# Negative maxima placed between down sums, a sum placed ahead of gelu's end, five places in each early section, and w_down loaded first

## The chip, the cores and the metric

The kernel runs on one core of a Trainium2 chip. The metric is the device time of one execution in microseconds (us). The core has five engines that run side by side and meet at semaphores: TensorE (PE in the profile, its weight loads PEld) multiplies matrices into PSUM, which has eight banks; VectorE (DVE), ScalarE (ACT) and GpSimd (POOL) work element by element; SyncE (SP) issues the DMAs here. Before the change the median of three runs is 2544.03 us (2543.72 to 2545.23).

## The reference

The input x is 2048 tokens of 576 values. One normalised copy of it feeds an attention block of 32 heads of 18 values and a GEGLU feed-forward block of 4608 hidden values. The result joins both:

```python
def _A_ref(x, wqkv, wo):
    ...
    scores = jnp.einsum("bhqd,bhkd->bhqk", q, k) * (Dh ** -0.5)
    p = _softmax(scores, axis=-1)
    o = jnp.einsum("bhqk,bhkd->bhqd", p, v)
    return (lambda x, *d: x.transpose(*d))(o, 0, 2, 1, 3).reshape(B, S, D) @ wo

def _B_ref(x, w_gate, w_up, w_down):
    return (_gelu(x @ w_gate) * (x @ w_up)) @ w_down

xn = _layernorm(x, axis=-1)
s = _A_ref(xn, A_wqkv, A_wo)
g = _silu(_B_ref(xn, B_w_gate, B_w_up, B_w_down))
return x + s * g
```

All inputs are float32. The kernel keeps that precision by splitting a value into a high part, rounded to the type fp32r that TensorE multiplies, and a low part, the rest.

## The kernel before

**Stages.** A prologue normalises x, transposes it and computes queries, keys and values into DRAM. Then come 144 sections (n = 0 to 143), and an epilogue that projects the attention's output and applies the gate.

**A section** (`section`) computes gate and up of 128 hidden values for one block of 512 tokens (`gate_up`): 27 pairs of matmuls, one on each half of the array's rows, into the PSUM tiles pg and pu. Other matmuls are spread between the pairs (`specials`). After it `activate` begins gelu: a square on ScalarE (L426), the product L427 on VectorE, and then, in the list `FF["rest"]`, `times` (a copy of pu on ScalarE, L435, and the product L438, which is the last to read pg) and `rest` (the tanh on ScalarE, L443, and gelu's last product L446 on VectorE). `finish` splits the hidden values into hh and hl, and after each second section it splits the two rows of w_down into dh and dl.

**A down product** (`down`, `half_downs`) multiplies the hidden values of two sections with their rows of w_down. It is cut into sums of 128 tokens by 288 columns, each accumulated in a PSUM tile py of one bank and then added by VectorE to the tile Y (`add_down`, L461; in the first rows of a block it is copied). Up to section 11 a run has four sums, two runs for each pair of sections; in the attention part it has eight, once for two sections. A sum is made of two halves, one on each half of the array; `behind` sets a mark on ScalarE after an opening half. The pieces of `FF["rest"]` are taken off at such marks, `times` at that of sum 0 and `rest` at that of sum `late` (1, or 2 in the last pair of a block).

**Attention** runs in 32 units (a block of 512 queries and four heads), four sections to a unit (n = 10 to 137, `ATT`). Before the exponentials the kernel needs the maximum of each row of scores, so the scores are multiplied twice: `max_mm` (L709, pm) with a maximum by VectorE (L712), and, five sections behind it, `score_mm` (L747, pe) with the exponential by ScalarE (L748). Eight slots of 32 make a section. `values` (L782, acc) runs after each second section. The first 40 slots of maxima lie ahead of the attention part, in the early sections: `FIRST` gives how many slots, called places here, each of the sections 0 to 9 takes. The last maximum of such a section waits until after L427 (`late`).

When the maxima of a unit are complete, `max_neg` forms the negative maxima on VectorE (L724), rounds them (the copy L725), subtracts to get the low part (L726), transposes both (L727) and stores them to DRAM (L728, mT). `max_rows` reads them back as rows of the query tiles (L736), so that the score matmul itself subtracts the maximum. In the attention part `max_neg` stands after each fourth section (12, 16, and so on to 132), ahead of that section's down product, and `max_rows` one section on. For the first unit both stand after section 8.

**Order.** The order on TensorE is that of the program text. On the other engines and on SP the build chooses an order by the text and the dependencies. Three helpers bind it: `tc.keep_in_program_order` and `kept` fix an instruction at its place, and `no_sync(a, b, ...)` puts a behind b on the engine without a semaphore; `after` is a real wait. SP is one queue, so a DMA that waits holds all behind it.

**Banks.** `BANKS` gives the eight banks to three tags: two to "f" (pg and pu), three to "m" (pm and acc) and three to "s" (pe). The sums of a down product borrow them: four sums as "smss", eight as "mmsmfmss".

**w_down.** `load_down` loads the rows of w_down for two sections when the second of them begins (L540). In the early sections its buffer is one of those of the exponentials (`lead_raw`).

## Time and profile before

| | |
|---|---|
| median of 3 runs | 2544.03 us (2543.72 to 2545.23) |
| the profiled execution | 2543.24 us |
| its span, first to last instruction | 2541.4 us |
| granted TensorE clock | 1.0 in the whole span |
| instructions | 63721 |
| DMA | 325.54 MB, 128 GB/s mean |

The page cuts the span into 40 slices and gives the busy share of each in tenths:

```profile
PE   9999999999999999999999999999999999999999
DVE  5316978888888888888888888888888888887277
ACT  3223467666667766667666667666666666676622
POOL 2127644555565554445565554554446555455575
PEclk9999999999999999999999999999999999999999
```

A slice is 63.5 us. The prologue takes the first three, the early sections lie in slices 4 and 5 (196.8 to 293 us), the attention part reaches from there into slice 38. In views by instruction, "x" is a count, the figure ahead of the bar says shapes, and the words in brackets or behind the last bar tell what ended the idle time of the engine. In the chain of waits each row is a start, a duration and the work that the chain ran through.

### The profile page before, as it was taken

The page shows a single profiled execution, that of the slowest core. Times are in us where ns is not written, and L with a number is a line of the kernel's source. Part 1 is how long each engine was busy: PE and PEld are TensorE (multiplying, and loading weights), DVE is VectorE, ACT ScalarE, POOL GpSimd, SP SyncE. Part 2 cuts the span into 40 slices and gives each one's busy share as a digit, 9 for nine tenths or more (in the row PEclk, how much of TensorE's full clock was granted, in tenths as well). Part 3 has the DMA queues.
Part 4 walks back from the last instruction along what each step waited for, and adds up shares of the span by engine and source line. Part 5 has one row for each costly group of instructions (what it writes and reads, how often), then busy time and mean ns, then how long its engine had stood idle before and what let it go on. Part 6 is the DMA issues. An engine that isn't in the chain of part 4 may idle for free.

```text
span 2541.4 us, 63721 instructions
## 1 busy us (share of the span) xinstructions
PE 2534.5 (100%) x24214; PEld 2022.0 (80%) x24214; DVE 1947.5 (77%) x3491; ACT 1563.5 (62%) x3098; POOL 1320.0 (52%) x1447
## 2 busy tenths in 40 slices
PE   9999999999999999999999999999999999999999
PEld 8889977777778877777777777777777777777698
DVE  5316978888888888888888888888888888887277
ACT  3223467666667766667666667666666666676622
POOL 2127644555565554445565554554446555455575
PEclk9999999999999999999999999999999999999999
DMA  8875444444464444444455444344446444443483
GB/s 267 266 242 151 110 107 104 110 103 110 108 155 114 109 103 110 113 113 111 111 129 142 111 109 108 105 104 112 108 112 157 111 110 109 107 109 97 116 238 109
DMA packets 398688, 325.54 MB, mean 128 GB/s; under 512 B 117408, under 2 KB 309184, under 8 KB 398384
## 3 DMA queue, kind: packets, MB, share of 16 engines
q1 hardware_dynamic: 398384, 321.47, 48.8%
q8 instruction: 193, 3.16, 0.5%
q14 instruction: 111, 0.91, 0.1%
HBM read 266.63 MB, written 54.70 MB: 126 GB/s over the span
## 4 chain that ended last, share of the span: by engine, by line
PE 98%; ACT 1%; DVE 0%; POOL 0%; issue 0%; POOLq 0%; ACTq 0%
PE pg L413 29%; PE py L473 18%; PE acc L782 18%; PE pm L709 9%; PE pe L747 9%; PE po L180 7%; PE pu L413 6%; PE po L921 2%; ACT pT L748 1%; PE pt L241 0%; PE po L232 0%; DVE t L446 0%; POOL dl L113 0%; POOL hl L113 0%; ACT t L426 0%
## 5 line engine op out<-in xcount | busy, mean ns | idle before, releaser
L748 ACT ACTIVATE pT<-pe 128x512 f32<-128x512 f32 x2048 | 1153.4, 598 | 364.6 <-PE pm L709 224.0
L712 DVE TENSOR_REDUCE mx<-pm 128x1 f32<-128x512 f32 x2048 | 1250.2, 682 | 148.2 <-PE pm L709 146.0
L413 PE MATMUL pu<-xd,wh 64*128 64x512 f32 x2592 | 925.9, 390 | 0.2 <-DVE t L438 0.2
L413 PE MATMUL pg<-xd,wh 64*128 64x512 f32 x2592 | 925.7, 390 | 0.0
L709 PE MATMUL pm<-KS,q 64*128 64x512 f32 x2048 | 779.2, 387 | 0.0
L747 PE MATMUL pe<-q,KS 64*128 64x512 f32 x2048 | 775.6, 387 | 0.9 <-DVE Y L461 0.9
L413 PEld LDWEIGHTS pg<-xd,wh 64*128 64x128 f32 x2592 | 476.9, 184 | 110.3 <-POOL wh L106 19.3
L413 PE MATMUL pg<-xd,wl 64*128 64x512 f32 x1296 | 501.3, 387 | 0.0
L413 PE MATMUL pu<-xd,wl 64*128 64x512 f32 x1296 | 501.3, 387 | 0.0
L413 PEld LDWEIGHTS pu<-xd,wh 64*128 64x128 f32 x2592 | 477.0, 184 | 1.1 <-DVE t L438 0.6
L782 PE MATMUL acc<-pT,VS 128*32 128x512 f32 x4096 | 452.8, 594 | 0.0
L108 POOL TENSOR_TENSOR wl<-raw,wh 128x384 fp32r<-128x384 f32 x432 | 433.4, 1016 | 14.0
L106 POOL TENSOR_SCALAR hh<-t 128x512 fp32r<-128x512 f32 x128 | 79.1, 618 | 663.3 <-DVE t L446 648.6
L709 PEld LDWEIGHTS pm<-KS,q 64*128 64x128 f32 x2048 | 374.9, 184 | 25.4 <-DVE mx L712 1.3
L747 PEld LDWEIGHTS pe<-q,KS 64*128 64x128 f32 x2048 | 370.5, 184 | 22.6 <-DVE Y L461 1.9
L473 PE MATMUL py<-dh,hh 64*128 64x288 f32 (+1 forms) x2240 | 366.0, 293 | 0.2
L473 PE MATMUL py<-dl,hh 64*128 64x288 f32 (+1 forms) x2240 | 365.3, 292 | 0.1
L473 PE MATMUL py<-dh,hl 64*128 64x288 f32 (+1 forms) x2240 | 364.5, 292 | 0.0
L782 PEld LDWEIGHTS acc<-pT,VS 128*32 128x32 f32 x4096 | 127.3, 110 | 289.9 <-issue 278.4
L106 POOL TENSOR_SCALAR wh<-raw 128x384 fp32r<-128x384 f32 x432 | 217.2, 514 | 137.6 <-PE pu L413 82.7
L461 DVE TENSOR_TENSOR Y<-py,Y 128x288 f32<-128x288 f32 x544 | 226.1, 452 | 53.5 <-PE py L473 46.3
L413 PEld LDWEIGHTS pg<-xd,wl 64*128 64x128 f32 x1296 | 238.6, 184 | 30.3
(120 smaller groups left out, 3135.3 us busy)
## 6 DMA issues: line engine op xcount, KB each, us to landing
KS<-qk SPq DMA_DIRECT2D x1536, 36.0 KB
raw<-in_B_w_gate_dram SPq DMA_DIRECT2D x144, 288.0 KB
raw<-in_B_w_up_dram SPq DMA_DIRECT2D x144, 288.0 KB
raw<-in_B_w_down_dram SPq DMA_DIRECT2D x67, 576.0 KB
VS<-vs SPq DMA_DIRECT2D x128, 152.0 KB
qk<-t SPq DMA_DIRECT2D x72, 256.0 KB
q<-qk SPq DMA_DIRECT2D x384, 36.0 KB
xx<-in_A_x_dram SPq DMA_DIRECT2D x32, 288.0 KB
```

Of the source, the lines that this page charges most:

```text
L106: first = nc.gpsimd.tensor_scalar(hi, raw, 1.0, 1.0, op0=ALU.mult, op1=ALU.mult)
L108: low_part[:] = [keep(nc.gpsimd.tensor_tensor(lo, raw, f(hi), op=ALU.subtract))]
L180: nc.tensor.matmul(o, st, m, start=(i == 0), stop=(i == len(terms) - 1))
L413: nc.tensor.matmul(o, w[1 + wp][k][rr, c, :], xd[xp][k][rr, c, :], start=(i == 0), stop=(i == len(terms) - 1))
L461: one = kept(nc.vector.tensor_tensor(yy, py, yy, op=ALU.add))
L473: return nc.tensor.matmul(py, hs[g][a][rr, j * P:(j + 1) * P], wd[w][rr, g, 288 * c:288 * c + 288], start=start, stop=stop)
L709: nc.tensor.matmul(pm, QS[u, r][rr, t * P:(t + 1) * P], KS[(u * NA + c) % KB][r][rr, :], start=True, stop=True)
L712: return nc.vector.tensor_reduce(MX[u][:, 2 * r + a, t, c:c + 1], pm, axis=AX.X, op=ALU.max)
L747: nc.tensor.matmul(pe, KS[(u * NA + c) % KB][r][rr, t * P:(t + 1) * P], QS[u, r][rr, :], start=True, stop=True)
L748: nc.scalar.activation(PT[u, kt][:, 2 * r + a, :], pe, AF.Exp, scale=SCALE)
L782: nc.tensor.matmul(ACC[u][32 * a:32 * a + 32, :], VS[(u * NA + c) % VB][:, v:v + 32], pt[:, a, :], start=first, stop=last, skip_group_chec ...
L921: nc.tensor.matmul(po, parts_of(b, j)[x_][:, k, :], OW[w][c][k], start=(i == 0), stop=(i == len(OUT) - 1))
```

## The change

Four edits and what they need. The order of gelu's pieces is taken apart: `tanh` and `rest` are now two entries of `FF["rest"]`. `max_neg` returns its four steps in place of doing them; the second is a second reduction of the maxima into the rounded tile, where a copy stood. The steps wait in `FF["between"]`: in runs of eight sums one is taken off after the third sum and two after the fourth, and what is left goes behind the last sum (`downs`). In runs of four sums nothing is taken off between the sums, and all four steps go behind the last. In runs of four, gelu's last product stands behind the first sum and ahead of the second. `FIRST` gives five places to each of the sections 2 to 9, where it gave 4, 5, 5, 5, 5, 5, 5, 6. The first rows of w_down are asked for ahead of the first keys and queries. For the first unit `max_rows` moves from right behind `max_neg` to the section's end.

```diff
-FIRST = (0, 0, 4, 5, 5, 5, 5, 5, 5, 6)
+FIRST = (0, 0) + (5,) * 8
...
-        def rest(behind=None, evicted=None):
-            tanh = kept(nc.scalar.activation(t1, t1, AF.Tanh, scale=GC * GS))
+        def tanh(behind=None, _=None):
+            one = kept(nc.scalar.activation(t1, t1, AF.Tanh, scale=GC * GS))
             if behind:
-                no_sync(tanh, behind, "a mark first")
+                no_sync(one, behind, "a mark first")
+
+        def rest(_=None, evicted=None):
             one = kept(nc.vector.scalar_tensor_tensor(t1, t1, 1.0, t2 if early else pg, op0=ALU.add, op1=ALU.mult))
             if evicted:
                 no_sync(one, evicted, "a finished sum first")
             if not early:
                 kept(nc.vector.tensor_tensor(t1, t1, pu, op=ALU.mult))
-
-        return t1, [times, rest] if early else [rest]
+            return one
+
+        return t1, [times, tanh, rest] if early else [tanh, rest]
...
-            one = kept(nc.vector.tensor_tensor(yy, py, yy, op=ALU.add))
+            one = FF["added"] = kept(nc.vector.tensor_tensor(yy, py, yy, op=ALU.add))
...
                             if begun == 0:
                                 evicted = add_down(b, r, pys[k], Y, j, c)
+                                if ahead:
+                                    no_sync(evicted, ahead, "between two finished sums")
+                                    ahead = None
+                                done += 1
+                                if done == 1 and len(sums) == 4 and len(FF["rest"]) == 1:
+                                    ahead = FF["rest"].pop(0)(None, evicted)
+                                for _ in range({3: 1, 4: 2}.get(done, 0) if len(sums) > 4 and FF["between"] else 0):
+                                    ahead = FF["between"].pop(0)(evicted)
                             elif a == 1 or len(sums) == 4:
                                 seen[k] = behind(one)
                                 if k in (0, late) and FF["rest"]:
-                                    FF["rest"].pop(0)(seen[k], evicted if k == 2 else None)
+                                    FF["rest"].pop(0)(seen[k])
+                                if k == late and FF["rest"] and len(sums) > 4:
+                                    FF["rest"].pop(0)(None, evicted if k == 2 else None)
...
-            FF["rawd"] = load_down(r, raw_d() if raw_d else raw_tile([P, G, D])) if ahead else FF.pop("next_d")
+            FF["rawd"] = FF.pop("first_d") if n < G else load_down(r, raw_d() if raw_d else raw_tile([P, G, D])) if ahead else \
+                FF.pop("next_d")
...
     def downs():
         while FF["down"] and (FF["down"][0][-1] < FF["n"] or FF["n"] == NF):
             down(*FF["down"].pop(0)[:-1])
+        while FF["between"]:
+            FF["between"].pop(0)(FF["added"])
...
-        def max_neg(u, keep=lambda i: i):
+        def max_neg(u):
...
-            keep(nc.vector.tensor_reduce(nm, MX[u].rearrange("p a t c -> p (a t) c"), axis=AX.X, op=ALU.max, negate=True))
-            nc.vector.tensor_copy(m2[:, 0:MH], nm)
-            nc.vector.tensor_tensor(m2[:, MH:2 * MH], nm, f(m2)[:, 0:MH], op=ALU.subtract)
-            nc.vector.transpose(m2t, f(m2))
-            nc.sync.dma_start(mT[u], m2t)
+
+            def step(what):
+                def go(behind=None):
+                    one = what()
+                    if behind:
+                        no_sync(one, behind, "a finished sum first")
+                    return one
+                return go
+
+            def square():
+                one = nc.vector.transpose(m2t, f(m2))
+                nc.sync.dma_start(mT[u], m2t)
+                return one
+
+            return [step(what) for what in (
+                lambda: nc.vector.tensor_reduce(nm, MX[u].rearrange("p a t c -> p (a t) c"), axis=AX.X, op=ALU.max, negate=True),
+                lambda: nc.vector.tensor_reduce(m2[:, 0:MH], MX[u].rearrange("p a t c -> p (a t) c"), axis=AX.X, op=ALU.max,
+                                                negate=True),
+                lambda: nc.vector.tensor_tensor(m2[:, MH:2 * MH], nm, f(m2)[:, 0:MH], op=ALU.subtract),
+                square)]
...
-            tc.keep_in_program_order(nc.vector.reciprocal(den, den))
+            one = nc.vector.reciprocal(den, den)
+            tc.keep_in_program_order(one)
+            no_sync(one, FF["added"], "finished sums first")
...
+        FF["first_d"] = load_down(0, lead_raw())
         for r in range(2):
             load_k(0, rs=(r,))
             load_q(0, (r,))
...
             if slot + m >= NS > slot:
-                max_neg(0, tc.keep_in_program_order)
-                max_rows(0)
+                FF["between"] = max_neg(0)
...
+            full = len(FF["between"]) > 0
             downs()
             run_rest()
             finish(cut=split_ap)
+            if full:
+                max_rows(0)
...
             if im == 0 and um <= NU:
-                max_neg(um - 1)
+                FF["between"] = max_neg(um - 1)
                 at(n + 1, 0, max_rows, um - 1)
```

More of the change, by code (lines that the diff above doesn't have):

```diff
@@ L391 @@
     copied.clear()
-    FF = {"w": ahead, "xd": XD, "down": [], "n": 0, "keep": None, "late": [],
+    FF = {"w": ahead, "xd": XD, "down": [], "n": 0, "keep": None, "late": [], "between": [], "added": None,
           "Y": ffn.tile([P, TB // P, D], F32, name="Y")}
@@ L490, in half_downs @@
         late = 2 if r == NR - 1 else 1
+        done, ahead = 0, None
         def downs_of(a, ks):
@@ L495, in step @@
                     def step(k=k, i=i):
-                        nonlocal evicted
+                        nonlocal evicted, done, ahead
                         j, c = sums[k]
@@ L832 @@
             lead = [lambda s=s: lead_pair(s, s == slot + m - 1) for s in range(slot, slot + m)]
-            section((1 + (n == 2)) * none * (m > 0) + lead, "s" if n == 1 else "f", lead_raw)
+            section((m > 0) * (1 + (n == 2)) * none + lead, "s" if n == 1 else "f", lead_raw)
             if slot + m >= NS > slot:
-                max_neg(0, tc.keep_in_program_order)
-                max_rows(0)
+                FF["between"] = max_neg(0)
             slot += m
```

## The prediction

> **What bounds the kernel now.** I read the page's busy times first, then the chain of waits.
>
> ```profile
> PE 2534.5 (100%) x24214; PEld 2022.0 (80%) x24214; DVE 1947.5 (77%) x3491; ACT 1563.5 (62%) x3098; POOL 1320.0 (52%) x1447
> ...
> PE 98%; ACT 1%; DVE 0%; POOL 0%; issue 0%; POOLq 0%; ACTq 0%
> ```
>
> The tensor engine is busy all the time and carries the chain. The change takes no matmul away, so only the places where a matmul starts late can be won. The chain in order of time shows the attention part as a beat of two sections: eight sums of a down product (py), then the values (acc).
>
> ```profile
> 374.13 6.36 PE py L473 x95
> 390.28 7.00 PE acc L782 x64
> 407.26 6.52 PE py L473 x93
> 423.54 7.00 PE acc L782 x64
> ...
> 2332.42 6.51 PE py L473 x96
> ```
>
> From py to acc it takes 16.15 us at 374.13 and 16.28 us at 407.26. The long ones (6.51 to 6.62) are 26 from 407.26 to 2332.42, not counting one at another kind of place. They are the down products that follow a section in which negative maxima are formed, one in four sections (31 such places; a few show no loss). So 0.13 us is lost at each. Asked for the stretch from 195 to 345 us, the same view shows where the early sections lose time:
>
> ```profile
> 216.73 3.38 PE py L473 x44
> ...
> 269.95 3.22 PE py L473 x46
> ...
> 280.50 0.61 ACT t L426
> ...
> 282.58 0.52 DVE m L725
> ...
> 283.54 0.58 DVE t L438
> 284.17 0.49 PE pu L413
> ...
> 292.44 0.78 PE py L473 x9
> ...
> 295.10 0.69 DVE t L446
> ...
> 296.21 0.50 PE pe L747
> ```
>
> A section of five places takes 10.55 us (269.95 to 280.50), and the next one 11.94 (280.50 to 292.44). There the four operations of `max_neg` stand on VectorE ahead of the product L438 that frees the gate banks, and PE waits until 284.17. At 296.21 a score matmul waits for the bank of a down sum, which VectorE adds only after gelu's last product L446.
>
> **The change part by part.**
>
> *Negative maxima between the sums.* The timelines of VectorE for the place at 407.26 and for the quiet one at 374.13, then of PE:
>
> ```profile
> 407.97 0.22 DVE L724 TENSOR_REDUCE nm<-mx 128x16 f32<-128x64 f32 x1
> ...
> 408.53 0.68 DVE L427 SCALAR_TENSOR_TENSOR t<-t,pg 128x512 f32<-128x512 f32 x1
> 409.13 0.20 DVE L727 STREAM_TRANSPOSE m2t<-m 128x32 f32<-128x32 f32 x1
> 409.25 0.65 DVE L438 TENSOR_TENSOR t<-t,pg 128x512 f32<-128x512 f32 x1
> ...
> 410.62 1.18 DVE L461 TENSOR_TENSOR Y<-py,Y 128x288 f32<-128x288 f32 x3
> 412.10 0.46 DVE L461 TENSOR_TENSOR Y<-py,Y 128x288 f32<-128x288 f32 x1 [0.30 <-PE py L473]
> 412.89 1.75 DVE L461 TENSOR_TENSOR Y<-py,Y 128x288 f32<-128x288 f32 x4 [0.34 <-PE py L473]
> ...
> 414.72 3.61 DVE L712 TENSOR_REDUCE mx<-pm 128x1 f32<-128x512 f32 x6
> ```
> ```profile
> 377.18 1.41 DVE L461 TENSOR_TENSOR Y<-py,Y 128x288 f32<-128x288 f32 x3
> ```
> ```profile
> 413.50 0.39 PE L413 MATMUL pg<-xd,wh 64*128 64x512 f32 x1
> 413.62 0.39 PE L413 MATMUL pu<-xd,wh 64*128 64x512 f32 x1
> ...
> 415.54 0.39 PE L709 MATMUL pm<-KS,q 64*128 64x512 f32 x1
> ```
>
> The first sum begins 3.36 us after its py row with the maxima ahead (407.26 to 410.62) and 3.05 without (374.13 to 377.18). The first sum's bank is needed again by the sixth sum, so one half of the array falls behind: pg and pu, which start together elsewhere, are 0.12 apart at 413.50. The values need both halves, and there the 0.13 is paid. With the operations moved, the first sum comes 0.31 earlier; more than the delay. Saved: 26 x 0.13 = 3.4.
>
> Where they go: one after the third sum, two after the fourth, the transpose after the last. The first three cost 0.56 on the engine (407.97 to 408.53); the idle gaps of 0.30 and 0.34 ahead of the fourth and fifth sum take them, so the fifth sum, whose bank the next gate needs at 413.50, is late by at most 0.1; it now ends near 413.35 (412.89 plus 0.46). The transpose adds 0.12 (409.13 to 409.25) between the last sum and the next maxima. Is that covered? The first maximum ends near 415.35 (414.72 plus some 0.63, from six in 3.61), and its bank is taken again at 415.54: 0.19 of cover. PE will be there 0.13 earlier, but the last sum too by about 0.16 (quiet place: the maxima begin right after the last sum). So about 0.1 stays. I give 0.25 back in all: -3.15. Bounds: -3.4, and 0 if that cover is gone at each place.
>
> The Trainium skill (VectorE: DVE Perf Modes, "The DRAIN you can't avoid") says the next operation does not start until the pipe of the one before is empty. The rows disagree: three sums take 1.18, a step of 0.37 where one lasts 0.45. By the rule the transpose would take its whole 0.20, 0.08 more than the rows say; with no cover left that is 2.1 at 26 places, and the sum below would be -3.2 in place of -5.3.
>
> *Without a cast.* A second reduction of 64 values in place of a copy of 16:
>
> ```profile
> L724 DVE TENSOR_REDUCE nm<-mx 128x16 f32<-128x64 f32 x32 | 7.0, 220 | 1.1
> ...
> L725 DVE CAST m<-nm 128x16 fp32r<-128x16 f32 x32 | 5.9, 185 | 1.1
> ```
>
> That is 35 ns more at each of 32, but it no longer waits for the first; zero, hidden in the gaps above (bound +1.1 without them). A reduction that writes the rounded type is not in the trace; between L724's 220 and the 520 of L725 at 282.58, I take 220, the same operation.
>
> *Section 9.* Its places go from six to five, section 2 from four to five. PE's matmuls stay the same in sum, each place one step of 0.23. Section 9 should come down from 11.94 towards the 10.55 of a five-place section, of which 0.23 is the place that moved and the rest the wait at 284.17. But VectorE now does the four operations (0.7 to 0.8) right ahead of section 9's maxima, and these hold two banks at a time; I leave 0.3 of stall there: 10.85, so -1.1. Section 2's extra place is covered by a wait that stands there already:
>
> ```profile
> 203.23 2.06 SPq L676 DMA_DIRECT2D KS<-qk  x6
> ...
> 208.21 0.41 SPq L540 DMA_DIRECT2D pT<-in_B_w_down_dram  x1
> ...
> 212.75 1.30 POOL L113 TENSOR_TENSOR hl<-t,hh 128x512 fp32r<-128x512 f32 x1 [2.81 <-ACT hh L112]
> 214.00 2.67 POOL L113 TENSOR_TENSOR dl<-pT,dh 128x1152 fp32r<-128x1152 f32 x1
> ```
>
> The first down goes on at 216.73, right behind dl's end at 216.67, which does not move; so section 2's 0.23 comes off that wait and costs nothing (+0.23 if the wait is gone). Together -1.1, bounds -1.4 (no stall left in section 9) and -0.2.
>
> *w_down first.* dl starts when GpSimd is through with hl, and hl waits for ScalarE's hh; w_down has landed before. So an earlier load wins nothing by itself: 0. It now goes ahead of the 28 loads of keys and queries for section 2's maxima, which leave at some 0.35 each (six in 2.06, the last right before 208.21) and so start one issue (0.41) later. Half of them, for the first place, have left by 203; section 2 runs from about 210 to the down product whose row is at 216.73, and its places stand in the later part. That is the cover; without it the 0.41 is paid once. Bounds -0.4 and +0.4, one issue either way.
>
> *A sum ahead of gelu's end.* This touches ten runs of four sums; in those up to section 9 PE waits for none of them. Those after sections 9, 10 and 11 do:
>
> ```profile
> 309.38 0.39 PE L413 MATMUL pu<-xd,wh 64*128 64x512 f32 x1
> ...
> 310.11 0.49 PE L747 MATMUL pe<-q,KS 64*128 64x512 f32 x1 [0.32 <-DVE Y L461]
> ...
> 330.93 0.49 PE L747 MATMUL pe<-q,KS 64*128 64x512 f32 x1 [0.32 <-DVE Y L461]
> ```
>
> At each the score matmul starts some 0.5 late (310.11 after a gate matmul at 309.38, where one step of 0.23 would do). With the first sum ahead of L446, its bank comes 0.6 earlier. Next late is the second score, whose bank waits for L446 and the second sum, and the fourth maximum, for VectorE's work in sum is the same: I keep 0.15 of stall at each and take -0.35 three times, -1.05; bounds -1.6 and 0. L446 itself ends 0.37 later, hidden: its reader, the split of the hidden values, is used one section on.
>
> *The queue of the maxima's rows.* The store of the maxima leaves SP about 5 us later in the attention part, and eight row loads behind it:
>
> ```profile
> 283.57 0.35 SPq L728 DMA_DIRECT2D mT<-m2t  x1
> 285.59 5.38 SPq L736 DMA_DIRECT2D q<-mT  x8
> 291.03 4.40 SPq L676 DMA_DIRECT2D KS<-qk  x12
> ```
>
> From the store to the last landing that is about 2.0 + 5.4 + 2.0 = 9.4 us (landing taken as the 2.0 between these rows). In the attention part the scores that use the rows start two sections on, over 16 us; 0. For the first unit VectorE does the same work in another order: L438's end at 284.12, 0.6 for L446 and four sums of 0.37 give 286.2 for the end of the transpose, and the rows are landed near 295.6. The first score now starts 3.8 after its section's py row (292.44 to 296.21), 0.5 of it wait; with that row at 291.3 it is wanted at 294.6, and the third score, the first to use the second half of the rows, some 1.4 later, at 296. That is the thinnest cover; I cost it at 0, and its loss in rival B.
>
> Sum: -3.15 - 1.1 - 1.05 = -5.3. The profiled execution took 2543.24 (span 2541.4 and 1.8 around it): 2537.9. The median of the runs is 0.8 above it, so the forecast is 2544.03 - 5.3 = **2538.7**.
>
> **The rivals.**
> A. The gain at the 26 places is handed back at the next maxima, since PE is earlier and VectorE is not. For: cover of 0.1 is little, and VectorE is dense there. Against: the last sums follow PE. Only the early part stays: 2544.03 - 2.15 = 2541.9.
> B. The first scores of section 10 wait for the maxima's rows: the twelve key loads (4.40 us on SP, behind the row loads at 291.03 now) come ahead of the rows in the new text. If they stand behind the store, the rows land at 300, not 295.6, and the third score, wanted at 296, is 4.0 late, once: 2542.7. Against: the key loads need not wait for the transpose, and can leave ahead of the store.
> C. Slower: VectorE becomes the bound at 31 seams. If the sums come without the gaps of 0.30 and 0.34, the operations push the last sum and the maxima: 0.68 in all (0.56 and 0.12) against 0.1 of cover is 0.58 x 31 = 18.0; 2544.03 - 5.3 + 18.0 = 2556.7. It turns slower once 0.17 of it lies open at each place (5.3 over 31), slower by 0.2% from 0.34. Against: the gaps are PE's own pace and stand at the quiet place too.
> That the change does not do what it says holds for w_down, and is in the sum at zero.
>
> **How the numbers follow.** This kernel's measurement tells about 0.2% (5.1 us) from no change, so faster means below 2538.9. Forecast 0.58, its own range 2536.5 to 2541, of which 0.48 faster and 0.10 same; A 0.14 and B 0.10, same; C 0.13, slower; 0.05 for every bound at its best (-3.4 - 1.4 - 1.6 - 0.4 = -6.8: 2537.2), faster. Faster 0.53, same 0.34, slower 0.13. The range reaches from 2535.5 to 2546, which leaves most of C out.
>
> **What would show it.** Right: the py rows after the maxima at 6.36 and pg with pu together behind them; the step at section 9 near 10.9; no wait of pe for Y at the starts of sections 10 to 12; mT's store right behind the last sum. Wrong: steps of 16.28 that stay (A), a wait of pe for a load of q at section 10 (B), sums L461 that wait for VectorE rather than for py (C).

## The result and the profile after

The changed kernel takes 2547.59 us (median, 2544.61 to 2551.74), the kernel before took 2543.9 (2542.97 to 2545.41) on the same chip. The ratio is 1.0014, 95% interval 1.0007 to 1.002: slower by 3.7 us, inside the 0.2% that count as no change. The forecast was 2538.7 with a range up to 2546: the result lies outside the range, and it moved the other way. Its times also spread more widely than before.

The profiled execution has a span of 2545.4 us, 3.9 more than before. To see where, I take the start of each section's square on ScalarE (L426) as a mark, so that a "step" is the time from one section's mark to the next, and subtract the steps before from those after. The table is worked out from these marks.

| stretch | after minus before, us | predicted |
|---|---|---|
| up to the first mark (prologue) | +0.79 | 0 |
| sections 1 to 13 | -1.96 | -2.15 |
| the two steps at each of the three changes of the token block | +2.08, +1.32, +1.47 | 0 |
| the 26 places (the steps that were long before) | -0.23 | -3.15 |
| all other sections | +0.45 | 0 |

The prologue is not part of the change. In the kernels below, which do not touch it either, it differs from the one before by -0.48 to +0.67 (and once by 2.3), so I leave it out. Of the 0.45 in the other sections, 0.40 stands in one step (section 95) where no other kernel here shows it. Two things have to be explained: 4.87 us lost at three places that the forecast did not look at, and 2.9 of the 3.15 us not won at the 26 places.

The chain by engine, from the page of the changed kernel:

```profile
PE 97%; ACT 1%; DMA 1%; DVE 0%; POOL 0%; issue 0%; SPq 0%; ACTq 0%; POOLq 0%
```

DMA has appeared in the chain with 1%; before it was not named.

**Early sections.** The marks of sections 8 to 10:

```profile
281.30 0.60 ACT L426 ACTIVATE t<-pg 128x512 f32<-128x512 f32 x1 [5.30 <-PE pg L413]
...
292.08 0.60 ACT L426 ACTIVATE t<-pg 128x512 f32<-128x512 f32 x1 [6.63 <-PE pm L726]
...
306.23 0.59 ACT L426 ACTIVATE t<-pg 128x512 f32<-128x512 f32 x1
```

Section 9 now takes 10.78 (281.30 to 292.08), section 10 14.15. By the same marks they took 11.93 and 14.02 before; sections 11 and 12 come to 13.32 for 13.79 and 20.50 for 20.89. In sum this part went nearly as forecast (-1.96 for -2.15), though section 10 became longer and not shorter.

**The 26 places.** The chain of waits of the changed kernel in the stretch from 400 us, in order of time:

```profile
406.06 6.36 PE py L476 x96
422.32 7.00 PE acc L814 x64
439.30 6.36 PE py L476 x95
455.47 7.00 PE acc L814 x64
```

The down product py after the maxima has come down to 6.36, as the forecast wanted. But from py to acc it is still 16.26 us (406.06 to 422.32), against 16.17 at the quiet place behind it. The loss has moved, to the seam behind py, where the sums end and the next section's gate matmuls begin. VectorE's timeline there:

```profile
409.11 1.41 DVE L464 TENSOR_TENSOR Y<-py,Y 128x288 f32<-128x288 f32 x3
410.43 0.21 DVE L756 TENSOR_REDUCE nm<-mx 128x16 f32<-128x64 f32 x1
...
411.23 0.21 DVE L757 TENSOR_REDUCE m<-mx 128x16 fp32r<-128x64 f32 x1
411.48 0.30 DVE L759 TENSOR_TENSOR m<-nm,m 128x16 fp32r<-128x16 f32 x1
411.70 1.57 DVE L464 TENSOR_TENSOR Y<-py,Y 128x288 f32<-128x288 f32 x4
```

The first sum starts 3.05 after its py row, as at a quiet place. The four operations stand where the change puts them. One row is odd: the difference L759 takes 0.30; before, the same operation took 0.175, as at this place:

```profile
408.44 0.17 DVE L726 TENSOR_TENSOR m<-nm,m 128x16 fp32r<-128x16 f32 x1
```

TensorE and its weight loads (PEld) at the seam, in the changed kernel, and then at the quiet place at 374.13 of the kernel before:

```profile
412.12 0.18 PEld L413 LDWEIGHTS pg<-xd,wh 64*128 64x128 f32 x1
...
412.20 0.18 PEld L413 LDWEIGHTS pu<-xd,wh 64*128 64x128 f32 x1
412.26 0.39 PE L413 MATMUL pg<-xd,wh 64*128 64x512 f32 x1
412.26 0.44 PE L413 MATMUL pu<-xd,wh 64*128 64x512 f32 x1
...
412.49 0.18 PEld L726 LDWEIGHTS pm<-KS,q 64*128 64x128 f32 x1
...
412.72 0.39 PE L413 MATMUL pg<-xd,wl 64*128 64x512 f32 x1
...
412.83 0.39 PE L413 MATMUL pu<-xd,wl 64*128 64x512 f32 x1
```
```profile
380.33 0.39 PE L413 MATMUL pg<-xd,wh 64*128 64x512 f32 x1
380.33 0.40 PE L413 MATMUL pu<-xd,wh 64*128 64x512 f32 x1
...
380.34 0.19 PEld L709 LDWEIGHTS pm<-KS,q 64*128 64x128 f32 x1
```

pg and pu now start together (412.26). Then the weights of the maxima's first matmul pm load 0.23 after them (412.49), where the quiet place needs 0.01 (380.34). pm starts late, the next pu too, and from there the halves of the array are 0.11 apart (412.72 and 412.83) until the values, where it is paid as before. Between them lie three semaphore instructions on TensorE's queue, at 412.198, 412.309 and 412.415. The programs' lists say what they wait for (buffer numbers left out):

```
before  L709 pm<-KS,q  [waits DMAHW7, DMAHW6, DMAHW0]
after   L726 pm<-KS,q  [waits DMAHW5, DMAHW4, DMAHW6, DMAHW3, DMAHW7, DMAHW2, DMAHW0]
```

At each of these places pm is the first reader of the next unit's queries and of new keys. Before, it waits on three DMA queues, afterwards on seven. It is not the data that is late: the last of the landings on these queues ahead of the seam is at 409.70, 2.5 us before the first of the three instructions.

**The changes of the token block.** The chain at the first of them:

```profile
723.53 11.03 DMA xd<-xhs
...
734.68 1.48 POOL xd L146
...
736.20 0.50 PE pu L413
```

TensorE waits for the new block of x (xd), which lands at 734.6 and is copied by GpSimd. SP, the queue that issues the DMAs, after and then before:

```profile
684.01 0.64 SPq L126 DMA_DIRECT2D raw<-in_B_w_gate_dram  x1
...
685.50 5.19 SPq L768 DMA_DIRECT2D q<-mT  x8
690.73 0.65 SPq L126 DMA_DIRECT2D raw<-in_B_w_up_dram  x1
...
701.05 0.65 SPq L126 DMA_DIRECT2D raw<-in_B_w_gate_dram  x1
...
703.52 0.58 SPq L554 DMA_DIRECT2D raw<-in_B_w_down_dram  x1
...
704.61 8.36 SPq L693 DMA_DIRECT2D KS<-qk  x12
...
719.25 2.60 SPq L142 DMA_DIRECT2D xd<-xhs  x4
```
```profile
685.15 0.66 SPq L126 DMA_DIRECT2D raw<-in_B_w_gate_dram  x1
685.86 0.63 SPq L126 DMA_DIRECT2D raw<-in_B_w_up_dram  x1
...
691.56 0.89 SPq L126 DMA_DIRECT2D raw<-in_B_w_up_dram  x1
...
707.59 4.23 SPq L676 DMA_DIRECT2D KS<-qk  x12
...
715.24 4.64 SPq L142 DMA_DIRECT2D xd<-xhs  x4
```

The store of the maxima is late, so its eight row loads come late, and now stand between a gate load and its up load. The next pair of raw loads leaves at 701 to 703, right ahead of w_down and the keys; before, its second half had left at 691.56. Behind these three large loads the twelve key loads take 8.36 us to leave, not 4.23, and the new x leaves 4.0 later. In the same queue fifteen of the sixteen query loads now follow the keys (713.00 to 718.03), of which twelve used to go ahead of them.

### The profile page after: what moved, and what is told of

It is laid out like the page before. It is cut to its first block, busy times and chain, and to the rows that moved or that the text cites. A ratio compares the mean times of both kernels' runs of the same rounds, so it can differ in the third digit from the quotient of the medians.

```text
span 2545.4 us, 63688 instructions
## 1 busy us (share of the span) xinstructions
PE 2536.4 (100%) x24214; PEld 2019.4 (79%) x24214; DVE 1955.1 (77%) x3491; ACT 1563.8 (61%) x3098; POOL 1323.4 (52%) x1447
## 4 chain that ended last, share of the span: by engine, by line
PE 97%; ACT 1%; DMA 1%; DVE 0%; POOL 0%; issue 0%; SPq 0%; ACTq 0%; POOLq 0%
PE pg L413 28%; PE py L476 18%; PE acc L814 17%; PE pm L726 9%; PE pe L779 9%; PE po L180 7%; PE pu L413 6%; PE po L958 2%; ACT pT L780 1%; DMA xd<-xhs 0%; PE pt L241 0%; DMA rawp<-in_A_wqkv_dram 0%; POOL xd L146 0%; DVE t L448 0%; DVE Y L464 0%
## 5 line engine op out<-in xcount | busy, mean ns | idle before, releaser
L476 PE MATMUL py<-dh,hh 64*128 64x288 f32 (+1 forms) x2240 | 357.4, 293 | 0.2
L476 PE MATMUL py<-dl,hh 64*128 64x288 f32 (+1 forms) x2240 | 356.4, 292 | 0.0
L476 PE MATMUL py<-dh,hl 64*128 64x288 f32 (+1 forms) x2240 | 356.3, 292 | 0.0
L464 DVE TENSOR_TENSOR Y<-py,Y 128x288 f32<-128x288 f32 x544 | 227.2, 451 | 41.3 <-PE py L476 33.7
```

What stands on the lines that cost most here:

```text
L464: one = FF["added"] = kept(nc.vector.tensor_tensor(yy, py, yy, op=ALU.add))
L476: return nc.tensor.matmul(py, hs[g][a][rr, j * P:(j + 1) * P], wd[w][rr, g, 288 * c:288 * c + 288], start=start, stop=stop)
```

## Experiments: the three changes of the block

**The maxima ahead again.** The change with one edit undone in the attention part:

```diff
-                FF["between"] = max_neg(um - 1)
+                for go in max_neg(um - 1):
+                    go()
```

> The changed kernel, but in the attention part the four operations of the maxima stand ahead of the down product again, as before; all other edits stay. Theory Q (the loss at the three changes of the token block comes from the order of SP's queue, which the later store of the maxima sets): the loss of 4.9 us there goes, the 26 long steps from py to acc go back to 16.28, and only the early gain of 2 stays: about 2542, below the kernel before. Rival V (the loss at the changes comes from another edit, w_down first or the sum ahead of gelu's end): the changes of block still cost 4.9 and the time stays near 2547.

Measured: 2539.8 us against 2543.57, ratio 0.9985 (0.9977 to 0.9994). The steps at the three changes differ from before by -0.01, 0.00 and 0.00. So the loss there belongs to the place of the maxima; the other edits, left as they are, do not make it. That it beats the forecast of 2542 by 2 us is a miss, taken up below.

**Nothing but the maxima between the sums,** on the kernel before (its `max_neg` and `half_downs` as in the changed kernel).

> The kernel before, with nothing but the four operations of the maxima between the sums in the attention part. Theory Q: 4.9 us are lost at the three changes of the token block and nothing is won at the 26 places (16.23 to 16.28): about 2549. Rival V: no loss at the changes: 2544, or 2541 if the places win.

Measured: 2549.15 against 2543.57, ratio 1.0022 (1.0013 to 1.003). The changes cost 3.44, 1.43 and 0.73 there, 5.6 in sum, and the 26 places give next to nothing (-0.09). This edit alone makes the loss. (The profiled execution took 2550.68; another 1.4 of it stands in section 5, which the edit does not touch.)

**Raw loads behind the rows of the maxima.**

```diff
+            rows = FF.pop("rows", None)
+            def behind_rows(i):
+                keep(i)
+                if rows:
+                    no_sync(i, rows, "rows of the maxima first")
-            nxt = load_gu((n + 1) % (NR * G), keep) if ahead else FF.pop("next_gu")
+            nxt = load_gu((n + 1) % (NR * G), behind_rows) if ahead else FF.pop("next_gu")
```

> The changed kernel, with the next raw gate and up loads ordered on SP behind the eight loads of the maxima's rows, so that these do not stand between the gate load and the up load. The operations on VectorE stay where the change put them. Theory Q: the wait for the new block of x at the three changes goes or shrinks to under 1 us, 2547.6 - 4.9 = 2542.7; the 26 places stay at 16.23 to 16.26. Rival V: the late store itself, not the order behind it, costs the 4.9: 2547 as it is.

Measured: 2553.51, ratio 1.0039 (1.0025 to 1.0052): a miss. At section 10 the edit holds the raw loads behind the first unit's rows, and that step grows by 7.9 us. At the three changes 0.40, 2.47 and 0.34 remain, 3.2 of 4.9: the raw pair still leaves just ahead of the keys (20.4 us before the mark of the last section, as in the changed kernel). Splitting gate from up was not the whole of it.

**The block of x ahead of the queries,** together with queries ahead of keys (next section). At a change of block the sixteen query loads are ordered behind the first load of xd (the lines that keep this load in `x_last` and pass `keep` on are left out here):

```diff
             if i == 1 and u + 2 < NU and new_x:
-                load_q(u + 2)
+                load_q(u + 2, keep=lambda one: no_sync(one, x_last[0], "x first"))
```

> The changed kernel with the queries ahead of the keys, and where the token block changes, the sixteen loads of the queries ordered on SP behind the loads of the new block of x. Theory Q: the block of x leaves SP some 5.8 us earlier, the wait of 3.7 us for it at the three changes goes: 2544.5 - 3.7 = 2540.8, below the kernel before. Rival (the transfers are late because they collide with the raw loads, wherever they stand in the queue): the wait stays, 2544.5.

Measured: 2541.14 against 2543.33, ratio 0.9991 (0.9982 to 1.0). The first four loads of x leave 7.3, 7.3 and 7.0 us before the mark of the section (before: 7.3 each; changed kernel: 2.2, 2.0, 2.4), and the changes cost 0.00, 0.30 and 0.28. With queries ahead of keys alone they cost 1.16, 1.16 and 1.44. The store of the maxima and the next raw pair leave as late as in the changed kernel (the gate load 20.2 to 20.4 us before the mark, there 20.4 to 20.7). But the twelve keys now start 3.2 to 4.8 us later and leave in 4.3 to 5.2 us, where they took 8.4 to 8.5. So with the store as late as it is, the order of the loads behind it on SP decides nearly all of the loss, and 0.6 of it stays. Which of these transfers holds up which is not separated.

## Experiments: the 26 places

Here the halves' distance is read behind the second gate matmul (pu minus pg), and py to acc from the chain, both at the place near 406 us; the time is that of the whole kernel.

| kernel | pm waits on | difference L759 | halves apart | py to acc | us |
|---|---|---|---|---|---|
| before | 3 queues | 0.175, ahead | 0.13 | 16.28 | 2543.9 |
| changed | 7 | 0.30 | 0.107 | 16.26 | 2547.6 |
| queries ahead of keys | 3 | 0.30 | 0.053 | 16.18 | 2544.5 |
| all four ahead | 3 | 0.175 | 0.07 | 16.19 | 2539.8 |
| difference behind the sixth sum | 3 | 0.85 | 0.012 | 16.83 | 2556.5 |
| a third reduction in its place | 3 | (0.21) | 0.013 | 16.17 | 2540.7 |
| only the transpose between the sums | 3 | 0.175 | 0.012 | 16.14 | 2538.5 |

**Queries ahead of keys.** Where the block does not change:

```diff
             if n > 0 and not new_x:
-                load_k(n - 1 + KB)
+                if i == 1 and u + 2 < NU:
+                    load_q(u + 2)
+                load_k(n - 1 + KB, lambda one: no_sync(one, FF["q"], "queries first") if i == 1 else None)
```

> The changed kernel, with the queries' loads ordered on SP ahead of the keys' loads of the same section, so that the first maximum's matmul of a unit (pm, right behind the down product) waits on three DMA queues and not on seven. Theory Q: the two halves of the array stay together behind the first gate matmul, the long steps from py to acc fall from 16.25 to about 16.16, 23 to 26 times 0.09 = 2.2 less: 2545.4; the loss at the changes of the block stays. Rival V (VectorE's operations make the fifth sum, whose bank the next gate needs, late): the steps stay at 16.25 and the time at 2547.6.

Measured: 2544.49 against 2543.57, ratio 1.0004 (0.9995 to 1.0013), 3.1 less than the changed kernel. Nothing on VectorE is moved, and the places fall by 0.08 in the median, mark to mark (16.24 to 16.16). In the profiles the 26 places give 1.5 of the gain and the changes of block 1.1; the rest lies in the prologue. Half of the 0.107 is the wait on four more queues. The other half stays.

**Without the cast alone,** on the kernel before:

```diff
-            nc.vector.tensor_copy(m2[:, 0:MH], nm)
+            nc.vector.tensor_reduce(m2[:, 0:MH], MX[u].rearrange("p a t c -> p (a t) c"), axis=AX.X, op=ALU.max, negate=True)
```

> The kernel before, with nothing but the second reduction in place of the cast. Theory N (the second reduction does not wait for the first, so the first sum of each down product behind the maxima comes 0.07 to 0.08 earlier, and the halves of the array are 0.07 apart, not 0.13): the 26 long steps fall from 16.24 to about 16.16, 2543.6 - 1.8 = 2541.8. Rival (as predicted, the price is nothing or 35 ns more per place): 2543.6 to 2544.7.

Measured: 2541.63 against 2543.33, ratio 0.9992 (0.9984 to 1.0001): 1.7 us, with an interval that just reaches no change; the steps agree with it place by place. VectorE's timelines of the kernel before and of the one with all four ahead show why:

```profile
408.23 0.17 DVE L725 CAST m<-nm 128x16 fp32r<-128x16 f32 x1
```

```profile
406.37 0.22 DVE L756 TENSOR_REDUCE nm<-mx 128x16 f32<-128x64 f32 x1
406.51 0.21 DVE L757 TENSOR_REDUCE m<-mx 128x16 fp32r<-128x64 f32 x1
...
406.85 0.68 DVE L427 SCALAR_TENSOR_TENSOR t<-t,pg 128x512 f32<-128x512 f32 x1
```

The second reduction starts 0.14 after the first; the cast began 0.25 after it (407.972 and 408.226). The chain is 0.08 shorter up to L427, the first sum comes that much earlier, and the halves are 0.07 apart. It is also the size of the gain that the forecast for the first run above lacked.

**Keys in eight transfers,** to bring pm down to two queues:

```diff
-                    for n_, i in enumerate((0, 1, 0)):
-                        keep(nc.sync.dma_start(kk[n_ * DH:(n_ + 1) * DH, :], qk[i, rows, cols]))
+                    keep(nc.sync.dma_start(kk[0:2 * DH, :], qk[:, rows, cols]))
+                    keep(nc.sync.dma_start(kk[2 * DH:3 * DH, :], qk[0, rows, cols]))
```

> The changed kernel with queries ahead of keys, the new block of x ahead of the queries, and each key tile loaded by eight transfers in place of twelve (the first two of every three merged), so that the first pm of a section waits on two DMA queues, not on three or seven. Theory Q: with seven queues the halves of the array part by 0.107 behind the first gate matmul, with three by 0.055; with two they stay within 0.03, and the 26 steps fall from 16.17 to about 16.13: 2541.1 - 1.0 = 2540.1. Rival (the rest of the step is VectorE's fifth sum): the steps stay at 16.17, 2541.1.

> As the one with eight key transfers, but the two reductions stand ahead of the down product and only the difference and the transpose between the sums, both behind the third: the store leaves some 2.7 us earlier than in the changed kernel. Theory Q: places as with eight transfers (16.13) if the first sum is now early enough, and no wait left at the changes of the block: about 2539.5. Rival: two reductions ahead still make the first sum late, halves 0.05 apart, 16.16: 2540.5.

Measured: 2586.68 and 2589.02, ratios 1.017 (1.0156 to 1.0184) and 1.0178 (1.0164 to 1.0192). Both miss: they take 43 to 45 us more than the kernel before, where the first of them without the merging is the kernel with x ahead, at 2541.14 (more in the last section). What they still tell: with two queues in place of three the halves are 0.04 to 0.05 apart at the places (0.05 with three), hardly less; so the rival in the expectation was right, and the rest is VectorE's. With the difference behind the third sum, in the second kernel, it takes 0.87 and the halves are 0.16 apart.

**The difference behind the sixth sum.** The steps of `max_neg` taken behind the third, fourth and sixth sum (`{3: 1, 4: 1, 6: 1}` in place of `{3: 1, 4: 2}`).

> As the kernel with the block of x ahead of the queries, but the difference of the two parts stands behind the sixth sum, no longer with the second reduction behind the fourth. Theory W (what is left of the long steps, 0.05 each, is the fifth sum, 0.04 late behind the difference, so that the weights of pu load late): the halves stay within 0.02 at the first gate matmuls, the 26 steps fall from 16.17 to about 16.13, 2541.1 - 1.0 = 2540.1. Rival (the rest is the waits on DMA queues alone): 0.055 apart and 16.17 as before, 2541.1.

Measured: 2556.48 against 2543.24, ratio 1.0051 (1.0038 to 1.0065). The time misses by 16 us, and yet theory W is shown in one respect: at the first five gate matmuls the halves are at most 0.029 apart, as at the quiet place. What went wrong stands in the timelines of VectorE and of GpSimd:

```profile
411.94 0.85 DVE L761 TENSOR_TENSOR m<-nm,m 128x16 fp32r<-128x16 f32 x1
```
```profile
411.74 1.99 POOL L108 TENSOR_TENSOR wl<-raw,wh 128x384 fp32r<-128x384 f32 x2
```

An operation on 16 values takes 0.85 us. It starts while GpSimd works on the first of two wl (411.743 to 412.765) and ends 0.03 after that operation's end.

**A third reduction in its place,** with the difference left out of the maxima's rows: the same place, one operand from SBUF in place of two.

```diff
-                lambda: nc.vector.tensor_tensor(m2[:, MH:2 * MH], nm, f(m2)[:, 0:MH], op=ALU.subtract),
+                lambda: nc.vector.tensor_reduce(m2[:, MH:2 * MH], MX[u].rearrange("p a t c -> p (a t) c"), axis=AX.X, op=ALU.max, negate=True),
```

> As the kernel with the difference behind the sixth sum, but a third reduction stands in the difference's place: the difference of the two parts is left out of the maxima's rows. Theory P (the difference reads two operands from SBUF and cannot end before the GpSimd operation in flight, which is why it takes 0.85 there; a reduction reads one): the operation takes 0.21, the 16.79 of the long steps falls to about 16.13, and the time to about 2540. Rival (the place behind the sixth sum is what costs, whatever stands there): still 0.85 and 2556.

Measured: 2540.65 against 2543.75, ratio 0.9986 (0.9977 to 0.9996). The operation:

```profile
411.70 0.21 DVE L761 TENSOR_REDUCE m<-mx 128x16 fp32r<-128x64 f32 x1
```

Theory P holds in this: 16 us hang on the operation, not on its place. The run exchanges the kind of operation together with the number of operands; other rows of the changed kernel tell the two apart. The sums L464, which read one operand from PSUM and one from SBUF, last 0.45 in the median, both where they start within a GpSimd operation (444 of them) and where they do not (100). Gelu's last product L448, which reads two from SBUF, lasts 0.69 alone; of the 38 that start within a GpSimd operation the median is 0.84 and the longest 1.52. So it is the second operand from SBUF. The median long step, mark to mark, is 16.20, not the 16.13 expected. Here the maxima begin behind the transpose, 7.44 after the py row (405.37 to 412.81); in the next kernel, with the transpose out of their way, it is 7.30 and the step is 16.12. That this is the rest is a reading: no run moves the transpose alone.

**Only the transpose between the sums.** The two reductions and the difference ahead of the down product, where GpSimd is idle; queries and x ordered as above.

```diff
-                FF["between"] = max_neg(um - 1)
+                *early, last = max_neg(um - 1)
+                for go in early:
+                    go()
+                FF["between"] = [last]
...
-                                for _ in range({3: 1, 4: 2}.get(done, 0) if len(sums) > 4 and FF["between"] else 0):
+                                for _ in range({3: 1, 4: 0 if alone else 2}.get(done, 0) if len(sums) > 4 and FF["between"] else 0):
```

> The changed kernel, queries ahead of keys and the block of x ahead of the queries, with the two reductions and the difference ahead of the down product, where GpSimd is idle, and only the transpose between the sums, behind the third. Theory P: the difference takes 0.175, the first sum comes 0.13 earlier than with all four ahead, the halves stay within 0.02, long steps 16.12 to 16.13, nothing lost at the changes of block: 2539.5 - 1.0 = 2538.5. Rival: the first sum is still late by 0.05 and nothing is won over all four ahead, 2539.5.

Measured: 2538.48 against 2543.75, ratio 0.9978 (0.9969 to 0.9987), the lowest of all, though its interval overlaps that of the kernel with all four ahead (0.9985, 0.9977 to 0.9994). VectorE at the place:

```profile
406.32 0.17 DVE L762 TENSOR_TENSOR m<-nm,m 128x16 fp32r<-128x16 f32 x1
...
408.41 1.28 DVE L465 TENSOR_TENSOR Y<-py,Y 128x288 f32<-128x288 f32 x3
409.61 0.20 DVE L754 STREAM_TRANSPOSE m2t<-m 128x32 f32<-128x32 f32 x1
```

The transpose lies in the gap ahead of the fourth sum, the halves stay together, py to acc is 16.14 (405.23 to 421.37), and the changes of block cost 0.01, 0.01 and 0.02.

## Experiments: the early sections, and all four ahead once more

The sum ahead of gelu's end was undone on the kernel with the maxima ahead (without the pop at `done == 1`, and with both parts of `rest` at `k == late`), and so was the early w_down load (`FF["first_d"]` removed).

> The kernel with the maxima ahead in the attention part, and the old order of gelu's end (no sum ahead of its last product in the runs of four). If the sum ahead is worth what the steps of sections 10 to 12 say: these steps come to 14.02, 13.79 and 20.89 as before, 0.76 more in sum. If that came from elsewhere: they stay at 14.12, 13.33 and 20.49.

> The kernel with the maxima ahead in the attention part, and the first w_down load in its old place. Forecast: steps of sections 2 and 3 within 0.1 of 7.68 and 10.63, so nothing in all. Rival: the early load lets the first down product start earlier, and undoing it costs up to 0.4.

Measured, one profile each: without the sum ahead the steps of sections 10 to 12 are 14.00, 13.69 and 20.90, 0.64 more in sum than with it (14.12, 13.32, 20.50). It is worth 0.77 in sections 11 and 12 and costs 0.12 in section 10. With w_down in its old place section 3 takes 10.80, not 10.62, and section 2 the same 7.68: 0.2, below what single profiles settle. In that profile dl waits 0.22 for ScalarE's dh, which it does not in the changed kernel. The whole kernels took 2539.98 and 2540.15.

> The kernel with the maxima ahead in the attention part once more, beside the other two on the same chip: 2539.8 as at first (0.9985 of the kernel before).

Measured: 2539.45, ratio 0.9983 (0.9975 to 0.9992).

## Why the prediction was wrong

**The queue of the maxima's rows** is the step that failed first. It asked when the rows are needed ("two sections on, over 16 us; 0") and stopped there. The rows were indeed in time. What it did not ask is what stands behind them on SP: raw loads, keys, queries and the new x, in one queue. This cost 4.87 us, where the forecast had 0; the nothing-but-this kernel and the one with x ahead show it from both sides. A look at what stands behind a moved store was taken for the first unit alone (rival B, which did not come).

**Negative maxima between the sums** was to bring -3.15 and brought -0.23. The observed cause was right: the first sum does come 0.31 earlier, py is 6.36, pg and pu start together. But a second and a third loss lay under the first, and the forecast read only the largest of the three. One half was the step that lets the idle gaps take the three operations, with the fifth sum "late by at most 0.1" and nothing charged for it. It took their 0.56 from a place where GpSimd is idle and the difference lasts 0.175. Between the sums the difference takes 0.30, and the fifth sum is 0.04 late (it starts at 411.702, released at 411.661). That is within the 0.1, but it is not free: the weights of pu, which wait for this sum's end, load 0.075 after those of pg, where 0.037 is the distance at places without the delay, and pm's weights follow later by as much. The other half was no step at all: the moved store turned the order of queries and keys, and pm's waits went from three queues to seven. In the kernel where neither arises, with only the transpose between the sums, py to acc is 16.14. The transpose took 0.12 up to the next operation (413.192 to 413.317), as the forecast read from its rows, and not its whole 0.20. Whether the 0.25 for the cover at the next maxima was enough stays open: with queries ahead of keys all that is left at a place, halves and cover together, is 0.035 (16.156 against 16.121 at the quiet places), but the kernel with a third reduction keeps 0.07 while its halves stay together.

**Without a cast** was costed at 0, bound +1.1. In the old place it is worth -1.7; in the new place no run separates it. The term compared durations (220 against 185) and not the dependency: a cast waits for its reduction, a second reduction does not.

**Section 9** came to 10.78 for 10.85, right; that it is so close is partly luck, since nine other kernels with the same text there give 10.59 to 11.00. **Section 2** with section 3 came to +0.05 for 0, and **w_down**, by one profile, to about -0.2 for 0. Both lie within their bounds. If the 0.2 is real, section 2's extra place was not free, and the two terms cancelled.

**A sum ahead of gelu's end** was right in mechanism and too large: -0.73 for -1.05 (0.64 by the kernel without it). The waits of pe for Y are gone. Sections 11 and 12 gave 0.47 and 0.39, where 0.35 each was reckoned; section 10 lost 0.13, because its score matmul now waits for ScalarE. The chain there:

```profile
296.22 1.15 ACT dh L112
297.37 0.49 ACT pT L780
297.90 0.49 PE pe L779
```

**The rivals.** A (places handed back, 2541.9) has the size of what the places did, by another way: not the next maxima, but the seam ahead of them. C (VectorE the bound) came in one kernel only, the one with the 0.85, near its price (2556.5 for 2556.7), by a mechanism that it did not contain, so that the agreement is luck. None of them held the loss at the block changes, so the range ended below the result. The four signs of being right all came (py at 6.36 with pg and pu together at their first matmuls, section 9, no wait of pe for Y, the store behind the last sum), but they lay where the forecast had looked. Of the signs of being wrong, that of A, steps that stay long, told of the places; none told of the changes of block. In the profile's own sum: 3.9 up in place of 5.3 down is 9.2, of which 4.87 are the changes, 2.9 the places, 0.45 the other sections, 0.79 the prologue and 0.2 the early sections.

## What to carry to other kernels

A store that leaves later is a new order for its queue. Before such a move is costed at nothing, list what stands behind it on that queue for the longest period of the kernel, and look at the reader of the last of them. A small stall read from the profile may lie over others of the same size: a gain is the difference to the next one, and a look at waits per matmul (how many queues) and at who else works at that moment (GpSimd) shows them. Price an operation in the company that it will have, not in the one that it had.

## What the runs showed of the hardware

**VectorE waits for GpSimd within an operation.** The difference of two operands from SBUF lasts 0.175 in all 32 places of the kernel before, where GpSimd is idle. In the changed kernel all 32 start within a GpSimd operation, 28 of them last 0.29 or more, and the median is 0.30; behind the sixth sum it is 0.84. Every stretched one ends 0.018 to 0.035 after the GpSimd operation's end. Reductions in the same company take 0.20 to 0.22, and so did the third reduction. The profile shows the stall as busy time, not as a wait. The Trainium skill (SBUF — State Buffer, "Who interferes with whom") says that a VectorE instruction with two inputs in SBUF contends with a GpSimd instruction that reads SBUF, that the one that comes second is blocked until the first is through, and that tensor_reduce on this chip never contends. The trace agrees on the two inputs (L759 and L448 against L464, above) and on the reductions. That it is blocked from its start to the other's end the rows do not show: it ends at most 0.035 after, and alone it takes 0.175.

**A wait on more queues is work for TensorE's queue.** Three semaphore instructions stand ahead of pm with seven queues, 0.11 apart, and its weight load comes 0.23 after that of pe (412.258 and 412.492), though the data has landed; with three queues, and no late sum, pm starts 0.01 behind its twin pe.

**Fewer transfers were slower.** Merging two key loads of 36 KB into one of 72 made the kernel 43 to 45 us slower than the one before. In sections 2, 3 and 5 alone it lost 16.7 (steps of 8.64, 16.87 and 20.03 for 7.11, 11.13 and 10.59), and the chain there holds landings of keys and raw loads:

```profile
220.51 8.53 DMA raw<-in_B_w_up_dram
229.05 8.19 DMA KS<-qk
```

The Trainium skill (DMA: Bandwidth & Descriptors, "Why a DMA increments its semaphore by 16 and not by 1") says that a copy runs on the largest number of engines, up to 16, that divides the slowest dimension of both its sides. The merged source begins with a dimension of 2, the single one with 18 rows; by that rule, as an estimate, 2 engines in place of 9. The landing events of the traces agree: behind a single load (issued at 404.04 in the changed kernel) the semaphore is raised at 404.50 and then nine times from 405.60 to 405.75; behind a merged one (at 214.16 in the kernel with eight transfers) at 215.27 and then twice, at 219.28 and 219.34.

**A lower clock after one stall.** In the kernel with the raw loads behind the rows, TensorE was busy for only 3.89 of the 9 us from 294 to 303; the granted clock was 0.90 in that stretch and 0.58 from 303 to 309, and it was 1.00 again from 309. This is one place in one profile. The window (its columns: the stretch, its length, busy time and count on PE, PEld, DVE, ACT and POOL, the granted clock, the DMA share, GB/s):

```profile
303.00:309.00 6.00, 5.78 (x32) 4.34 (x32) 3.32 (x5) 2.97 (x5) 6.00 (x7) 0.58 0.03 5
```
